# An attention and mixture-of-experts kernel: the exponential moves into the copy out of PSUM, and the list of steps is a new one

## The chip, the cores and the metric

The kernel runs on one core of a Trainium2 chip. The metric is the device time of one execution in microseconds (us). Engines are named as the profile names them: PE is TensorE's matmul side and PEld its weight loads, DVE is VectorE, ACT is ScalarE, POOL is GpSimd, SP is SyncE, which here only issues DMAs.

## The reference

```python
def _attn_ref(q, k, v):                       # q, k, v: 8 batches, 8 heads, 576 tokens, 64 wide, float32
    q_c = q.reshape(B, H, nc, chunk, D)       # nc = 9 chunks of 64 tokens; so are k_c, v_c
    scores = scale * np.matmul(q_c, k_c.transpose(0, 1, 2, 4, 3))      # scale = 1/8
    scores = scores - np.max(scores, axis=-1, keepdims=True)
    attn = np.exp(scores)
    attn = attn / (np.sum(attn, axis=-1, keepdims=True) + 1e-09)
    out = np.matmul(attn, v_c)
...
def _moe_ref(x, w_group, w_expert, w1, w2):   # x: 4608 tokens, 512 wide
    g_logits = x @ w_group                    # softmax over 4 groups, argmax: one group per token
    ...
        e_logits = xg @ w_expert[g]           # softmax over the group's 4 experts, argmax: one expert
        ...
            h = np.maximum(xg[mask_e] @ w1[g, e], 0.0)                 # 512 to 1024
            ye = h @ w2[g, e]                                          # 1024 to 512
            out[tok_idx] = (g_w[mask_g][mask_e] * e_w[mask_e])[:, None] * ye
```

## The kernel before, in words

The first part is attention with the routing of the tokens, the second runs the experts over the routed tokens. The second part ("units", one expert with up to 256 tokens each) is the same code before and after. The change lies in the first part.

Attention is cut into 36 tiles of 128 tokens: two chunks of 64 tokens, all eight heads. Each tile t goes through steps that have one letter each.

- **Q** loads the q and k of two tiles into a buffer `qk` (three buffers in turn); **V** loads the v of one tile with two or more copies into one of three blocks (`w1r`, `w2r`, `vg`; the first two hold weights later). Both go through SP's queue.
- **a** (`stage_a`, even numbers) turns q and k of a tile on PE, 16 transposes into a PSUM tile `tp`, of which there are two. ACT and DVE copy the halves to `qT` and `ktb` (line 419).
- **b** (`stage_b`) multiplies q with k into the PSUM tile `sc`, of which there is one. **s** (`stage_sub`) takes the row maxima on DVE (`m`) and writes the differences to `pr` in SBUF, which frees `sc`.
- **e** (`stage_exp`, line 452) takes the exponential of `pr` in place on ACT, with the scale of 1/8.
- **c** (`stage_ct`) turns `pr` on PE into a `tp`, often together with the output `x` of an earlier tile, and ACT copies it to `pT` (line 468).
- **p** (`stage_pv`) multiplies `pT` with v into the PSUM tile `o`; the v has a column of ones, so that a row of `o` also carries the row's sum. **n** (`stage_norm`) divides by it on DVE and writes `x`.
- **x** copies the turned `x` to `xT` on ACT (line 513). For every four tiles, steps written as digits and l, m and E follow: the router's logits, the choice of the expert, the rank of each token. **o** (on POOL) scatters the tokens to the experts' rows in HBM.
- **Z** fills spare rows in HBM from a tile of zeros, `pad` (five copies of 257 KB on SP's queue). P, j, J, X, U, L, H, D, W, w, y, F and R load and prepare the weights and run the first layer of the first expert.

No planner decides the order of these steps at run time or build time. `ORDER` is a string with all of them, and `run(ORDER)` records them one after the other; on each engine the instructions stand in this order, and wait for each other through semaphores. On SP's queue each copy besides waits until the copy eight before it has landed. An `a` with an odd number only forces a copy of the tile before it that is still owed; where nothing is owed it records nothing.

Of the kernel before, what the change touches and what calls it, by code (L numbers as in the profile page):

```python
# [13 lines left out]
AF = mybir.ActivationFunctionType  # L14
# [25 lines left out]
E1 = E + 1  # L40
NB0, NL0 = 2, 3
PB = (1, 3)
ORDER = ("a15 Q0 a19 a0 Q1 a6 a2 C0 G0 Q2 b0 a4 a11 a3 s0 a57 o0 a5 a13 b1 V0 e0 V2 a8 s1 c0 e1 b2 V1 a10 V3 p0 Q3 V7 G1"
# [17 lines left out]
FOUR = 16  # L61
VB = (0, 1, 0, 1, 0, 2, 1, 2, 2)
WHY = "the value comes from a table that the kernel builds within these bounds"
# [47 lines left out]
def moe_kernel(tc, q, k, v, w_group, w_expert, w1, w2, cst, out):  # L111
    nc = tc.nc
    w1 = w1.rearrange("g e d f -> (g e) d f")
    w2 = w2.rearrange("g e f d -> (g e) f d")
    with ExitStack() as ctx:
# [20 lines left out]
        x1 = xpool.tile([P, NG, XW], F32, name="x1", tag="x1")  # L136
# [7 lines left out]
        e0 = wpool.tile([1, 1], I32, name="e0")  # L144
# [88 lines left out]
        def prep_lo(i, eng=nc.gpsimd):  # L233
            h, l, r = prep_part(i, True)
            eng.tensor_sub(l, r, h.bitcast(F32))
# [5 lines left out]
        with ExitStack() as c1:  # L241
# [27 lines left out]
            st, TL = {}, NT - 1  # L269
# [81 lines left out]
            def flip(*parts):  # L351

                pt = banks().rearrange("p r (s c t) -> p r s c t", s=2, c=4)
                for i, f in enumerate(parts):
                    for c in range(4):
                        for r in range(2):
                            nc.tensor.transpose(pt[:, r, i, c], f(c)[HALF[r]], ident[HALF[r], HALF[r]])  # L357
                return [pt[:, :, i].rearrange("p r c t -> p c r t") for i in range(len(parts))]
# [88 lines left out]
                more(3)  # L447
                s["pr"] = pr

            def stage_exp(t):  # L450
                pr = st[t]["pr"]
                nc.scalar.activation(pr, pr, AF.Exp, scale=0.125)

            done = []

            def turned(t):
                o = st[t]["x"]
                return lambda c: o[:, c * P:(c + 1) * P]

            def stage_ct(t):  # L460
                pr = st[t]["pr"]
                parts = [lambda c: pr[:, c].rearrange("p x k -> p (x k)")]
                if done and done[0] <= t - 2:
                    o = done.pop(0)
                    parts.append(turned(o))
                pts = flip(*parts)
                pT = apool.tile([P, 4, P], F32, name="pT")
                nc.scalar.copy(pT.rearrange("p c (r t) -> p c r t", r=2), pts[0])
                st[t]["pT"] = pT
                if len(pts) > 1:  # L470
                    owed["x", o] = made[0], lambda: copy_x(o, pts[1])
# [37 lines left out]
            def copy_x(t, pt):  # L509
                g, i = divmod(t, NG)  # L510
                if i == 0:
                    st["xT", g] = xtpool.tile([P, 4, NG * P], F32, name="xT")
                nc.scalar.copy(st["xT", g][:, :, i * P:(i + 1) * P].rearrange("p c (r t) -> p c r t", r=2), pt)

            def stage_e1(g):
                xT = st["xT", g]
                lt = bank(g >= GL - 1)
                for c in range(4):
                    apart(mate[0], nc.tensor.matmul(lt[32 * c:32 * c + 32, :], lhsT=wg[:, c, :], rhs=xT[:, c, :], start=True, stop=True))
                st["lt", g] = lt, mate[0]  # L520

            def stage_lts(g):
                lts = xtpool.tile([P, 512], F32, name="lts")
                lt, h = st["lt", g]
                apart(h, nc.scalar.copy(lts, lt))
                st["lts", g] = lts

            def stage_e2(g):
                lts = st["lts", g]
                lg = lgk  # L530
                for i in range(NG):
                    nc.tensor.matmul(lg[:, i * 20:i * 20 + 20], lhsT=lts[:, i * P:(i + 1) * P],  # L532
                                     rhs=cs[:, C_SEL:C_SEL + 20], start=True, stop=True)
                st["lg", g] = lg
                routing.append(route(g))
# [249 lines left out]
            def prep2_lo(i, eng=nc.gpsimd):  # L785
                eng.tensor_sub(late2(4 + i // 2)[:, i % 2], w2r[i // K2][:, i % K2], hi2(0, i).bitcast(F32))
# [7 lines left out]
            def more(n=1):  # L794

                for _ in range(n):
                    while routing and next(routing[0], True):
                        routing.pop(0)
# [25 lines left out]
            def run(seq):  # L824
                g = dict(P=prep_hi, j=prep_lo, J=lambda i: prep_lo(i, nc.vector), X=first_x, U=first_xl, E=exponent, L=first_l1, H=first_hi, D=first_lo, W=prep2_hi, w=prep2_lo, y=lambda i: prep2_lo(i, nc.vector), F=first_loads, R=reload, V=load_v, C=load_cst,
                         Q=load_qk, G=load_wg, Z=prefill, a=stage_a)
                f = dict(o=stage_o, b=stage_b, s=stage_sub, c=stage_ct, e=stage_exp, p=stage_pv, n=stage_norm, x=stage_xt)
                for z in seq.split():
                    if z[0] == "m":
                        more(int(z[1:]))  # L830
                    elif z[0] in g:
                        g[z[0]](int(z[1:]))
                    elif z[0] == "1":
                        stage_e1(int(z[1:]))
                    elif z[0] == "l":
                        stage_lts(int(z[1:]))
                    elif z[0] == "2":
                        stage_e2(int(z[1:]))
                    elif z[0] == "3":
                        stage_e3(int(z[1:]))  # L840
                    elif 0 <= int(z[1:]) < NT:
                        f[z[0]](int(z[1:]))

            with tc.manual_schedule(engines={mybir.EngineType.PE, mybir.EngineType.DVE, mybir.EngineType.Activation, mybir.EngineType.SP, mybir.EngineType.Pool}):
                run(ORDER)
                while due:
# [22 lines left out]
        co, a, na, s4, thr, end = ft(2, "co"), ft(RPE, "a"), ft(2, "na"), ft(4, "s4"), ft(1, "thr"), ft(1, "end")  # L869
        ge, ff, ee = ft(U, "ge"), ft(U, "ff"), ft(E1, "ee")  # L870
        mk, rw = (ft(2 * U, n).rearrange("p (a u) -> p a u", a=2) for n in ("mk", "rw"))
        nd, thr2, bo, rv, rp, cd, pr = ft(1, "nd"), ft(1, "thr2"), ft(1, "bo"), ft(2, "rv"), ft(1, "rp"), ft(2, "cd"), ft(1, "prow")
        a64, nh, lf, th2 = ft(RPE, "a64"), ft(1, "nh"), ft(1, "lf"), ft(1, "th2")
# [814 lines left out]
```

## Time and profile before

| what | value |
|---|---|
| median of 3 runs (range) | 626.41 us (626.09 to 626.8) |
| profiled execution: time, and span of its instructions | 624.71 us, 623.1 us |
| mean granted clock of TensorE | 0.989 of full speed |
| ACT, busy time of the exponentials (line 452) | 22.4 us in 36 instructions |

The span runs from the first instruction to the last. The attention part fills about its first 183 us; from there the units run, with PE busy almost all of the time. An engine's busy time says little by itself; what counts is which wait ends last in a stretch.

### The profile page before, as it was taken

How to read it: one execution, taken by the hardware profiler on the slowest of the kernel's cores; microseconds unless marked ns; L12 is line 12 of the kernel's file. 1: busy time of each engine (PE TensorE's matmuls, PEld its weight loads, DVE VectorE, ACT ScalarE, POOL GpSimd, SP SyncE). 2: the span in 40 equal slices, each digit the busy share in tenths (PEclk: the TensorE clock that was granted, in tenths of full speed). 3: DMA queues.
4: the chain of work that ended last, by engine and by line, in shares of the span. 5: the costliest groups of instructions: out<-in, count | busy, mean ns of one | idle time of the engine just before them, and what ended most of it. 6: DMA issues, size and time to landing. Idle time of an engine off the chain costs nothing.

```text
span 623.1 us, 15370 instructions
## 1 busy us (share of the span) xinstructions
PE 593.3 (95%) x4882; PEld 502.0 (81%) x4883; DVE 428.8 (69%) x718; ACT 343.4 (55%) x521; POOL 220.6 (35%) x427
## 2 busy tenths in 40 slices
PE   3889999998999999999999999999999999999995
PEld 2777788777788888889888898888889888888884
DVE  4868889878868967427588876564844888966321
ACT  2878888888643835226375763534434575653311
POOL 9102555678861413113225232221311324323120
PEclk9889999999989999999999999999999999999998
DMA  9998999998548969213659667171721868741110
GB/s 224 239 280 227 285 284 277 273 259 250 180 181 262 395 206 351 85 51 95 243 229 343 241 243 266 62 291 43 272 99 38 304 241 277 288 166 67 34 37 31
DMA packets 104589, 128.00 MB, mean 205 GB/s; under 512 B 49438, under 2 KB 72222, under 8 KB 104544
## 3 DMA queue, kind: packets, MB, share of 16 engines
q1 hardware_dynamic: 93504, 92.71, 48.7%
q0 software_dynamic: 11040, 34.69, 15.6%
q8 instruction: 27, 0.44, 0.3%
q14 instruction: 18, 0.15, 0.1%
HBM read 106.23 MB, written 21.54 MB: 205 GB/s over the span
## 4 chain that ended last, share of the span: by engine, by line
PE 83%; DMA 6%; DVE 3%; ACT 3%; issue 3%; SPq 2%; DVEq 0%; POOL 0%; ACTq 0%; POOLq 0%
PE py L1047 29%; PE ph L1033 14%; PE ph L1015 7%; PE pxt L1033 6%; PE tp L357 5%; PE o L480 4%; PE sc L435 4%; DMA qk<-in_k_dram 3%; PE lgk L1033 3%; PE py L1064 2%; PE pxt L933 2%; DMA qk<-in_q_dram 2%; PE py L988 2%; PE lgk L532 1%; ACT qT L419 1%
## 5 line engine op out<-in xcount | busy, mean ns | idle before, releaser
L1589 POOL DMA_INDIRECT out_dram<-xl,io x37 | 41.6, 1125 | 155.4 <-DVE xl L1292 146.6
L1033 PE MATMUL ph<-xt,w1h 128*128 128x512 f32 (+1 forms) x280 | 73.2, 383 | 0.5 <-DVE htl L1345 0.5
L1223 ACT ACTIVATE hth<-ph 128x512 fp32r<-128x512 f32 (+1 forms) x28 | 16.1, 575 | 104.1 <-PE ph L1033 104.1
L1302 DVE TENSOR_TENSOR w1l<-w1r,w1h 128x2048 fp32r<-128x2048 f32 x28 | 64.0, 2291 | 8.5 <-ACT w1h L1199 7.5
L1047 PE MATMUL py<-w2h,hth 128*128 128x512 f32 x264 | 67.9, 399 | 0.0
L1047 PE MATMUL py<-w2h,htl 128*128 128x512 f32 x264 | 65.2, 389 | 0.0
L1306 DVE TENSOR_TENSOR w2l<-w2r,w2h 128x1024 fp32r<-128x1024 f32 x52 | 60.3, 1217 | 0.6 <-ACT w2h L1241 0.4
L1047 PEld LDWEIGHTS py<-w2h,htl 128*128 128x128 f32 x264 | 49.6, 188 | 10.3
L1047 PE MATMUL py<-w2l,hth 128*128 128x512 f32 x228 | 57.4, 390 | 0.0
L1047 PEld LDWEIGHTS py<-w2h,hth 128*128 128x128 f32 x264 | 47.3, 188 | 10.2 <-ACT hth L1277 1.2
L1199 ACT CAST w1h<-w1r 128x2048 fp32r<-128x2048 f32 x28 | 53.2, 1909 | 2.9 <-issue 1.5
L1033 PEld LDWEIGHTS ph<-xt,w1h 128*128 128x128 f32 x280 | 48.3, 189 | 6.7 <-DVE htl L1345 0.7
L1292 DVE TENSOR_SCALAR xl<-py,io 128x512 f32<-128x512 f32 x33 | 24.6, 748 | 42.0 <-PE py L1047 41.7
L1203 ACT CAST w2h<-w2r 128x2048 fp32r<-128x2048 f32 x28 | 52.3, 1929 | 0.0
L1047 PEld LDWEIGHTS py<-w2l,hth 128*128 128x128 f32 x228 | 42.8, 188 | 9.5
L1583 POOL COPY ion<-x1r 128x2 int32<-128x2 int32 x22 | 6.2, 281 | 119.0 <-PE pxt L933 119.0
L1274 ACT ACTIVATE xl<-ph 128x512 f32<-128x512 f32 x16 | 9.6, 599 | 69.3 <-PE ph L1015 69.3
L1033 PEld LDWEIGHTS ph<-xt,w1l 128*128 128x128 f32 x280 | 42.6, 189 | 4.9 <-DVE w1l L1302 0.3
L419 ACT COPY qT<-tp 64x512 f32<-64x512 f32 x56 | 36.7, 655 | 15.9 <-PE tp L357 14.6
L1033 PE MATMUL ph<-xt,w1l 128*128 128x256 f32 (+1 forms) x280 | 44.0, 278 | 0.1
L1333 DVE TENSOR_TENSOR xl<-ph,xl 128x512 f32<-128x512 f32 (+1 forms) x28 | 18.5, 661 | 35.2 <-ACT xl L1223 33.9
L357 PE MATMUL tp<-cs,qk 64*128 64x64 f32 x576 | 28.3, 242 | 13.6 <-DMA qk<-in_q_dram 8.6
(322 smaller groups left out, 1314.3 us busy)
## 6 DMA issues: line engine op xcount, KB each, us to landing
w2r<-in_moe_w_dram SPq DMA_DIRECT2D x30, 1024.0 KB, 7.5
w1r<-in_moe_w_dram SPq DMA_DIRECT2D x29, 1024.0 KB, 4.9
x1r<-xs POOLq DMA_DIRECT2D x38, 257.0 KB, 3.3
qk<-in_q_dram SPq DMA_DIRECT2D x15, 512.0 KB
qk<-in_k_dram SPq DMA_DIRECT2D x15, 512.0 KB
w1r<-in_v_dram SPq DMA_DIRECT2D x24, 128.0 KB
w2r<-in_v_dram SPq DMA_DIRECT2D x24, 128.0 KB
w1r<-in_moe_w_dram POOLq DMA_DIRECT2D x3, 1024.0 KB, 12.4
```

What stands on the lines that cost most here:

```text
L357: nc.tensor.transpose(pt[:, r, i, c], f(c)[HALF[r]], ident[HALF[r], HALF[r]])
L419: y.append((nc.vector.tensor_copy if not i and (z or a and FOUR <= n < 8 * B) else nc.scalar.copy)(to, at))
L435: nc.tensor.matmul(sc[HALF[c], hp], lhsT=st["T", u, 0][:, hp, c0 + j:c0 + j + CH], rhs=kt[:, hp, :, k0 + j:k0 + j + CH], start=True, stop= ...
L480: nc.tensor.matmul(o[HALF[c], hp // 2, hp % 2 * 2 * W:hp % 2 * 2 * W + 2 * W], lhsT=pT[:, hp, HALF[c]], rhs=s["va"][:, c, hp].rearrange("p ...
L1015: m = pe.matmul(ph[n], a_[:, c, 0:P], w_[:, c, n * 512:(n + 1) * 512], start=(i == 0), stop=(i == 11))
L1033: m = pe.matmul(o2 if i < 4 else o[:, 0:n], (w1l if i > 3 else w1h)[:, c, f * P:(f + 1) * P], both[:, c, :, 0:n] if i < 4 else xth()[:, c, ...
L1047: m = pe.matmul(py[j], a_[:, f, half[j]], w_(b, f), start=(i == 0), stop=(i == 23))
L1199: lambda b, s, j: ac.copy(wt[b][0][:, s], w1r[j]), K1, js)
L1203: lambda b, s, j: ac.copy(wt[b][2 + j], w2r[j]), K2)
L1302: lambda b, s, j: ve.tensor_sub(wt[b][1][:, s], w1r[j], wt[b][0][:, s].bitcast(F32)), K1, js)
L1306: m = ve.tensor_sub(wt[b][4 + 2 * j + i], w2r[j][:, 2 * i:2 * i + 2], wt[b][2 + j][:, 2 * i:2 * i + 2].bitcast(F32))
L1589: gp.indirect_dma_start(out, bass.IndirectOffsetOnAxis(ap=io[0:n, j, 0:1].bitcast(I32), axis=0), yb[0:n, j, :], None, bounds_check=N - 1, ...
```

## The change

`stage_exp` goes. `stage_ct` now turns the differences themselves, and the copy out of PSUM becomes an activation: ACT reads `tp`, applies the scale and the exponential, and writes `pT`. The letter e disappears from the list of steps, and the list is another one.

```diff
-ORDER = ("a15 Q0 a19 a0 Q1 a6 a2 C0 G0 Q2 b0 a4 a11 a3 s0 a57 o0 a5 a13 b1 V0 e0 V2 a8 s1 c0 e1 b2 V1 a10 V3 p0 Q3 V7 G1"
...
+ORDER = ("Q0 a5 a0 Q1 a6 a2 b0 C0 Q2 a19 V0 V2 V1 x2 a31 a61 V3 Q3 a4 G0 m1 x33 a8 V7 s0 V5 b1 c0 s1 b2 a10 s2 p0 Q4 a3 G1"
...
-            def stage_exp(t):
-                pr = st[t]["pr"]
-                nc.scalar.activation(pr, pr, AF.Exp, scale=0.125)
-
...
-                nc.scalar.copy(pT.rearrange("p c (r t) -> p c r t", r=2), pts[0])
+                nc.scalar.activation(pT.rearrange("p c (r t) -> p c r t", r=2), pts[0], AF.Exp, scale=0.125)
...
-                f = dict(o=stage_o, b=stage_b, s=stage_sub, c=stage_ct, e=stage_exp, p=stage_pv, n=stage_norm, x=stage_xt)
+                f = dict(o=stage_o, b=stage_b, s=stage_sub, c=stage_ct, p=stage_pv, n=stage_norm, x=stage_xt)
```

Line numbers after the change are five lower.

**ACT, the first tiles.** This is ACT's queue from the first copy into `ktb` to the second tile's `pT`, before:

```order
L419 COPY ktb_131<-tp 64x4x128
L419 COPY qT<-tp 64x4x128 x2
L419 COPY ktb_131<-tp 64x4x128
L452 ACTIVATE pr<-pr 128x512
L419 COPY qT<-tp 64x4x128 x2
L468 COPY pT<-tp 128x512
L452 ACTIVATE pr<-pr 128x512
L419 COPY ktb_132<-tp 64x4x128
L419 COPY qT<-tp 64x4x128 x2
L468 COPY pT<-tp 128x512
```

and after, from the same copy:

```order
L418 COPY ktb_131<-tp 64x4x128
L418 COPY qT<-tp 64x4x128 x2
L802 CAST tri<-cs 128x128
L803 CAST base<-cs 2x16
L418 COPY qT<-tp 64x4x128 x2
L418 COPY ktb_131<-tp 64x4x128
L463 ACTIVATE pT<-tp 128x512
L418 COPY ktb_132<-tp 64x4x128
L418 COPY qT<-tp 64x4x128 x2
L463 ACTIVATE pT<-tp 128x512
```

The activations of `pr` are gone, and each `pT` is written by an activation; two small casts stand later.

**SP, up to the sixth q and k.** The rows below end with the pair of q and k that is called Q5, for tiles 10 and 11; the pair further up is Q4. Before:

```order
L805 DMA wg<-in_moe_w_expert_dram 128x4x4 x2
L290 DMA qk<-in_q_dram 128x4x256
L290 DMA qk<-in_k_dram 128x4x256
L311 DMA w2r<-in_v_dram 64x8x64 x2
L819 DMA xs<-pad 128x514 x2
L311 DMA w2r<-in_v_dram 64x8x64 x2
L819 DMA xs<-pad 128x514
L311 DMA w2r<-in_v_dram 64x8x64 x2
L290 DMA qk<-in_q_dram 128x4x256
L290 DMA qk<-in_k_dram 128x4x256
```

and after:

```order
L310 DMA w2r<-in_v_dram 64x8x64 x4
L289 DMA qk<-in_q_dram 128x4x256
L289 DMA qk<-in_k_dram 128x4x256
L800 DMA wg<-in_moe_w_expert_dram 128x4x4
L310 DMA w2r<-in_v_dram 64x8x64 x2
L800 DMA wg<-in_moe_w_expert_dram 128x4x4
L310 DMA w2r<-in_v_dram 64x8x64 x2
L814 DMA xs<-pad 128x514
L289 DMA qk<-in_q_dram 128x4x256
L289 DMA qk<-in_k_dram 128x4x256
```

The same 16 copies of v stand ahead of Q5 (eight of them for `w1r`, further up in both), but one copy of `pad` in place of three; the other two follow Q5.

**SP, tiles 12 to 23.** The rows go from v for `w2r` past the pairs Q10 (the first q and k) and Q11 to Q13 (the last). Before:

```order
L311 DMA w2r<-in_v_dram 64x8x64 x6
L290 DMA qk<-in_q_dram 128x4x256
L290 DMA qk<-in_k_dram 128x4x256
L311 DMA w1r<-in_v_dram 64x8x64 x2
L290 DMA qk<-in_q_dram 128x4x256
L290 DMA qk<-in_k_dram 128x4x256
L311 DMA w1r<-in_v_dram 64x8x64 x6
L290 DMA qk<-in_q_dram 128x4x256
L290 DMA qk<-in_k_dram 128x4x256
L311 DMA vg<-in_v_dram 64x8x64 x8
```

and after:

```order
L310 DMA w2r<-in_v_dram 64x8x64 x2
L289 DMA qk<-in_q_dram 128x4x256
L289 DMA qk<-in_k_dram 128x4x256
L310 DMA w2r<-in_v_dram 64x8x64 x4
L310 DMA w1r<-in_v_dram 64x8x64 x2
L289 DMA qk<-in_q_dram 128x4x256
L289 DMA qk<-in_k_dram 128x4x256
L310 DMA w1r<-in_v_dram 64x8x64 x6
L310 DMA vg<-in_v_dram 64x8x64 x6
L289 DMA qk<-in_q_dram 128x4x256
L289 DMA qk<-in_k_dram 128x4x256
```

Q10 has passed four copies of v for `w2r`, and Q13 stands behind six copies of v for `vg` that followed it before.

## Rows read from the trace of the kernel before

**Rows 1.** Stretches: start:end, length, busy us (instructions) by engine; clock, DMA share, GB/s.
```profile
25.00:50.00 25.00, 21.27 (x372) 17.71 (x370) 18.70 (x38) 20.07 (x35) 0.00 (x0) 0.93 1.06 269
50.00:150.00 100.00, 96.47 (x1689) 79.03 (x1685) 86.94 (x209) 85.80 (x153) 59.77 (x168) 1.00 0.99 266
183.00:623.00 440.00, 432.75 (x2299) 369.52 (x2299) 284.34 (x376) 207.39 (x278) 119.20 (x189) 1.00 0.53 187
```

**Rows 2.** The chain that ended last: start, length, what.
```profile
34.37 8.11 DMA qk<-in_k_dram
...
71.93 5.64 DMA qk<-in_k_dram
...
121.51 11.18 DMA qk<-in_q_dram
```

**Rows 3.** Waits of PEld, 43 to 165 us: for whom, us in total, times, longest.
```profile
PEld tp L357 <- ACT ktb L419: 2.1, 4, 0.8
PEld tp L357 <- ACT xT L513: 1.8, 7, 0.4
PEld tp L357 <- ACT w2h L783: 1.7, 2, 0.9
PEld o L480 <- ACT pT L468: 1.6, 3, 0.8
PEld tp L357 <- ACT qT L419: 1.0, 2, 0.8
PEld sc L435 <- ACT pr L452: 0.8, 1, 0.8
```

**Rows 4.** Waits of PE, 43 to 183 us.
```profile
PE tp L357 <- ACT xT L513: 0.5, 2, 0.3
PE o L480 <- ACT pT L468: 0.5, 2, 0.3
PE tp L357 <- DMA qk<-in_k_dram: 0.4, 1, 0.4
```

**Rows 5.** ACT's groups: busy us, mean ns of one, idle before them.
```profile
L452 ACT ACTIVATE pr<-pr 128x512 f32<-128x512 f32 x36 | 22.4, 631 | 1.4 <-DVE pr L446 1.3
L468 ACT COPY pT<-tp 128x512 f32<-128x512 f32 x36 | 20.9, 586 | 10.2 <-PE tp L357 8.7 <-PE o L480 0.7 <-ACT lts L525 0.2
L1274 ACT ACTIVATE xl<-ph 128x512 f32<-128x512 f32 x16 | 9.6, 599 | 69.3 <-PE ph L1015 69.3
```

**Rows 6.** Timeline of the first 43 us: start, length, instructions, idle before and its end.
```profile
18.05 1.45 PE L435 MATMUL sc<-ktb,qT 128*64 128x128 f32 x16 [1.55 <-DVE pr L446]
...
40.14 0.46 PE L357 MATMUL tp<-cs,qk 64*128 64x64 f32 x8 [0.17 <-ACT xT L513]
...
42.53 1.55 PE L357 MATMUL tp<-cs,qk 64*128 64x64 f32 x24 [1.93 <-DMA qk<-in_k_dram]
```

**Rows 7.** SP's issues to DMA queues: start, length, copies.
```profile
27.50 1.09 SPq L819 DMA_DIRECT2D xs<-pad  x2
...
30.72 1.38 SPq L819 DMA_DIRECT2D xs<-pad  x1
...
34.37 0.51 SPq L290 DMA_DIRECT2D qk<-in_k_dram  x1
...
62.37 8.85 SPq L311 DMA_DIRECT2D w2r<-in_v_dram  x6
...
85.96 0.51 SPq L290 DMA_DIRECT2D qk<-in_k_dram  x1
86.56 9.75 SPq L311 DMA_DIRECT2D vg<-in_v_dram  x8
```

**Rows 8.** DMA issues: copies of the spare rows, KB each.
```profile
xs<-pad SPq DMA_DIRECT2D x5, 257.0 KB
```

**Rows 9.** PE's timeline where it first needs Q13 (the row of qk).
```profile
101.28 1.11 PE L480 MATMUL o<-w1r,pT 128*64 128x130 f32 x16
102.33 0.71 PE L357 MATMUL tp<-cs,qk 64*128 64x64 f32 x16
```

33 rows, old and new, of the table ORDER are left out of this document.

## The prediction

> **What bounds the kernel now.** I began with busy times by stretch [rows 1]. From 183 us on the code is the same in both kernels, and PE is busy for 432.75 of 440 us: that part keeps its length and only starts sooner or later. So the question is when the first 183 us end. Between 50 and 150 us the reader is to see four things almost full at once: PE 96.47 of 100, DVE 86.94, ACT 85.80, and the DMA engines at a share of 0.99 with 266 GB/s. No single one bounds; each waits for another now and then.
>
> Next I read the chain that ended last [rows 2]. Most of it is PE, but three long pieces are loads of q or k: one of 8.11 us that ends at 42.48, one of 5.64 us, one of 11.18 us. So the front of the kernel is set by what SP's queue brings, and the middle partly.
>
> Then I asked for whom PE waits. PE's own rows from 43 to 183 us put only 1.0 us on ACT's copies [rows 4]. Its weight loads, from 43 to 165 us, wait 9.0 us for ACT in the six groups shown, and 1.4 us in six smaller ones (`pT` 0.4, and five of 0.2), 10.4 us together [rows 3]. The two differ by ten, and the price of the whole change hangs on which is taken. Each small matmul here has its own weight load and cannot start without it, and ends of matmuls are modelled, so that an idle PE of some 0.2 us is covered in its rows. Between 50 and 150 us the weight loads are busy 79.03 us where PE shows 96.47 [rows 1]: there is more room than PE's rows say. I take 10.4 us as the most that ACT can give back there, and 1.0 us as the figure by PE's rows.
>
> The Trainium skill ("Trainium Kernel Development and Optimization", Performance Expectations) says the same of traces in general: matmul busy time is a bad measure because matmuls are pipelined, and the busy share of the weight loads a good one. By the matmul rows the term for ACT below would be at most 1.0 us; by the weight loads' rows it is up to 10.4. This trace's gap between 96.47 and 79.03 agrees with the page.
>
> **The change, step by step.**
>
> *The exponentials go.* 36 instructions of 631 ns, 22.4 us of ACT [rows 5]. From 50 to 150 us one is taken from ACT for each tile, some 24 tiles, so 24 x 0.63 = 15.1 us: ACT's 85.80 fall to 70.7, and its idle time doubles from 14.2 to 29.3. With twice the gaps in its queue I would expect about half of PE's waits for ACT to go, 5.2 us. But DVE, at 86.94, keeps all its work and is then the fuller of the two that empty PSUM; tiles that come faster meet it more often. I take 3.0 us, which is a choice; the bounds are 0 and 10.4.
>
> *The copy becomes an activation.* 36 copies of 586 ns [rows 5]. The trace has no exponential out of PSUM of this size. Bounds: 586 (as the copy), and 631, the exponential from SBUF. The nearest row is the Relu of line 1274, same size and out of PSUM, 599 ns. I take that: 13 ns x 36 = 0.5 us on ACT, at most 45 x 36 = 1.6. Only part of ACT's time reaches PE, 10.4 us of waits in 122 us; I put 0.1 us on the path (0 to 0.5).
>
> *The first tiles.* Without the exponential a tile's scores reach its `pT` some 0.6 us sooner, and in the new list PE turns the q and k of a further tile ahead of the second tile's scores, where it idled 1.55 us for DVE [rows 6]. I cost both at nothing, because what hides them is a load: PE is ready for Q5 at 40.14 and stands until 42.53 for its k [rows 6]. Whatever is won before waits there. If the load were not late, they would be worth up to about 2 us.
>
> *Q5 comes sooner.* SP's queue issues without a break up to Q5's k at 34.37 [rows 7], and the copies are the brake: a DMA share of 1.06 at 269 GB/s from 25 to 50 us [rows 1]. In the new list two of the three copies of `pad` stand behind Q5, and the 16 copies of v ahead of it are the same. That is 2 x 257 KB [rows 8] = 0.53 MB, at 269 GB/s 2.0 us. The issue times give nearly the same: two of three copies in 1.09 + 1.38 us [rows 7] are 1.6. I take 2.0 us. Bounds: 0, if Q4, which now stands behind two more copies of v, makes PE late instead; 3.7, if the granted clock, 0.93 in that stretch [rows 1], gives back its 7% of 25 us as well. I don't count on the clock, since PE still arrives before Q5 does. The two copies behind Q5 now stand ahead of Q6, but after 43 us PE's only wait for a k is one of 0.4 us [rows 4].
>
> *Q10 passes four copies of v.* Six copies take 8.85 us to issue [rows 7], so four are 5.9 us; the 0.4 us that PE waits for a k after 43 us [rows 4], at the end of the 5.64 us piece [rows 2], goes. Bounds 0 and 0.4.
>
> *Q13 falls behind six copies of v.* 9.75 us for eight [rows 7], so 7.3 us. Its k was issued at 85.96 [rows 7] and PE first needs it at 102.33 [rows 9]; the new issue is at about 93.3. PE will be there 2.0 + 0.4 and some 1.3 of the 3.0 us sooner, at 98.6. With 5.64 us from issue to landing [rows 2] it is there at 98.9, 0.3 us late. I count 0, and price the worse case below.
>
> *The end of the part.* Routing, first layer of the first expert and hand-over are the same instructions in nearly the same order; I count 0, with 1 us either way.
>
> **Sum.** -3.0 + 0.1 - 2.0 - 0.4 = -5.3 us. The profiled execution took 624.71 us, so 619.4. Its time lies 1.70 under the median of the runs, 626.41; so the runs should show 626.41 - 5.3 = **621.1 us**.
>
> **Rivals.**
>
> *The waits change their owner.* ACT's waits go, and PE waits for DVE, or for DMA, instead. For it: DVE is as full as ACT was, and the DMA share is 0.99 [rows 1]; then the 2.0 us of Q5 are also handed back at the next load. Against it: Q5's delay is a delay of copies that nothing needed early. Between nothing and the 0.4 of Q10 plus half of the 2.0 would be left, 0 to 1.4 us: about 625.7, no change that can be measured.
>
> *Q13 comes too late (slower).* If Q13's k takes the 11.18 us of the chain's third load [rows 2] and not 5.64, it lands at 93.3 + 11.2 = 104.5, 5.9 us after PE wants it. That eats the 5.3 us and 0.6 more; and after so long a stall the clock would fall as in the stretch of the earlier one, 0.93 for 25 us, another 1.75 [rows 1]. 626.41 + 2.3 = 628.7. It decides from a landing of some 11 us on. For it: the queue has eight copies under way, and six of them are now copies of v just issued. Against it: the chain's other two loads took 5.64 and 8.11 us; with 8.11 PE would wait 2.8 us, and the kernel would still be faster.
>
> *All of it.* Both doubts resolve well: PE's whole 10.4 us go and the clock's 1.75 are given back. -5.3 - 7.4 - 1.75 = -14.4, 612. Against it: PE is at 96.47 of 100 even so, and v and k must come at a rate that is already 266 GB/s. Half of the extra, some 616.5, is as far as I go.
>
> That the change does not do what it says can be left out: the activations of `pr` are gone from ACT's queue.
>
> **How the numbers follow.** A measurement of this kernel tells about 0.2% from no change, 1.25 us. Forecast, between 1.25 and 9 us gained: 0.67. All of it: 0.04. Waits that change their owner: 0.17. Q13 late: 0.12. So faster 0.71, same 0.17, slower 0.12. The range: below, 616.5 keeps half of the extra gain; above, 626.7 takes in the second case whole and cuts the third. The forecast's own range is 617.4 to 625.
>
> **What would show it.** ACT's groups: line 463 with 36 instructions at about 600 ns, no exponential of 128x512 besides; ACT's busy time some 22 us less. The wait for a k near 42.5 us ends near 40.5. The weight loads' waits for ACT's `ktb`, `pT` and `xT` are together a third less. The wait for Q10's k is gone, and one for a k near 98 us is below 1 us. From the start of the units to the end, 440 us as before. It would be wrong if PE's waits for DVE grow by what those for ACT lose, or if SP's queue shows a long wait for a buffer in front of a pair of q and k.

## The result, and the profile after

The changed kernel takes 628.76 us (median of 14 runs; the kernel before, run beside it, 624.1): a ratio of **1.0076 [1.0049, 1.0103]**. It is slower, where 621.1 us and faster was forecast (0.992 of the 626.41 us that were known then). In two later groups of runs the same kernel gave 1.0052 [1.0021, 1.0084] and 1.0067 [1.0039, 1.0095]. The profiled execution took 628.77 us, with a span of 627.1 us.

First the busy times by stretch, as in [rows 1] (stretch and its length; PE, PEld, DVE, ACT, POOL; granted clock, DMA share, GB/s):

```profile
25.00:50.00 25.00, 19.21 (x330) 15.74 (x332) 16.90 (x33) 14.96 (x25) 0.00 (x0) 0.93 0.95 248
50.00:150.00 100.00, 93.55 (x1645) 77.63 (x1643) 84.69 (x202) 72.76 (x125) 57.66 (x165) 0.99 1.03 265
183.00:623.00 440.00, 435.80 (x2328) 372.38 (x2323) 286.68 (x384) 207.91 (x280) 120.00 (x192) 1.00 0.54 188
```

Between 50 and 150 us ACT fell from 85.80 to 72.76 us, as meant. But PE fell too, from 96.47 to 93.55: it is idle 3 us more there, with ACT idle for 27 of 100 us. The DMA engines are as full as before.

The moved exponential has the size that was expected of it, 598 ns (the groups of ACT, as [rows 5]):

```profile
L463 ACT ACTIVATE pT<-tp 128x512 f32<-128x512 f32 x36 | 21.4, 598 | 19.6 <-PE tp L356 18.2 <-PE o L475 1.0
```

PE's weight loads wait less for ACT, too (43 to 165 us, as [rows 3]; smaller groups left out):

```profile
PEld tp L356 <- ACT xT L508: 3.2, 8, 0.8
PEld tp L356 <- ACT qT L418: 1.6, 2, 0.8
PEld tp L356 <- ACT ktb L418: 1.2, 4, 0.4
PEld tp L356 <- ACT pT L463: 1.1, 2, 0.8
```

With all groups of `xT`, `qT`, `ktb` and `pT` taken together that is 7.5 us where the kernel before had 7.3; what is gone is the exponential's share and nearly all of the weights' (`w2h`). The waits for ACT are about 8 us in all against 10.4.

Where the loss lies is told by one row of PE's timeline, the first matmul of the units. It stands in the kernel before at

```profile
199.42 1.12 PE L1033 MATMUL ph<-xt,w1h 128*128 128x512 f32 x4
```

and in the changed kernel at

```profile
203.42 1.12 PE L1028 MATMUL ph<-xt,w1h 128*128 128x512 f32 x4
```

4.0 us later, which is the whole difference of the spans (627.1 - 623.1): the units themselves are as long as before, and everything was lost in the attention part. This start of the units is used below as the yardstick for a trace. It holds for one execution only: three traces of the changed kernel lie 2.2 us apart (203.42, and 205.01 and 202.85 further below).

PE's timeline shows four places where it now stands. In each row the bracket is the idle time ahead and what ended it.

```profile
42.52 0.97 PE L356 MATMUL tp<-cs,qk 64*128 64x64 f32 x24 [0.96 <-DMA qk<-in_k_dram]
45.27 1.39 PE L514 MATMUL lgk<-xT,wg 128*32 128x512 f32 x8 [1.77 <-DMA wg<-in_moe_w_expert_dram]
...
112.72 0.40 PE L356 MATMUL tp<-cs,pr 64*128 64x64 f32 x6 [1.46 <-issue]
...
146.19 0.25 PE L356 MATMUL tp<-cs,qk 64*128 64x64 f32 x1 [0.83 <-DMA qk<-in_k_dram]
147.14 0.43 PE L356 MATMUL tp<-cs,qk 64*128 64x64 f32 x7 [0.71 <-DMA qk<-in_k_dram]
```

At 42.5 us it waits for Q5 as before. At 45.3 it waits for the last two copies of the router's weights. At 111.3 it stops in the middle of a group of eight transposes, for nothing that the profile names. At 146 to 147 it waits for Q17, the last q and k. None of the last three was in the prediction. The other two traces of this kernel show the same stop, but not the same waits after 43 us: after_again waits 1.1 us for the router's weights and not for Q17, after_third 2.5 and 1.9 us. SP's issues show why the two waits came:

```profile
19.32 3.06 SPq L807 DMA_DIRECT2D wg<-in_moe_w_group_dram  x1
...
34.24 0.60 SPq L289 DMA_DIRECT2D qk<-in_k_dram  x1
34.89 1.49 SPq L814 DMA_DIRECT2D xs<-pad  x2
36.42 3.31 SPq L800 DMA_DIRECT2D wg<-in_moe_w_expert_dram  x2
...
123.39 13.63 SPq L310 DMA_DIRECT2D vg<-in_v_dram  x8
137.11 2.21 SPq L299 DMA_DIRECT2D qk<-in_q_dram  x4
```

Q5's k is issued at 34.24 us, against 34.37 in [rows 7]: not 2 us sooner, though two pads moved behind it. The queue stood 3.06 us at a tiny copy of weights (G0), which the new list puts there. That is a part of it at most, for in the trace of after_third the stand is shorter and Q5's k still comes only 0.5 us sooner:

```profile
19.46 1.34 SPq L807 DMA_DIRECT2D wg<-in_moe_w_group_dram  x1
...
33.86 0.61 SPq L289 DMA_DIRECT2D qk<-in_k_dram  x1
```

Fewer bytes did not take less time. These are the stretches from 20 to 34.3 us, before and after (as [rows 1]):

```profile
20.00:34.30 14.30, 13.55 (x244) 11.73 (x240) 12.16 (x23) 13.34 (x22) 0.00 (x0) 0.93 1.05 259
20.00:34.30 14.30, 12.47 (x234) 10.82 (x236) 11.73 (x23) 10.46 (x17) 0.00 (x0) 1.00 0.90 215
```

At 215 instead of 259 GB/s some 0.63 MB less moved in the same time, about the two pads (0.53 MB) that were taken out.

The router's weights (G3, G4) now stand behind Q5 and two pads and are issued at 36.42, not 34.92. The new list also asks for them sooner: PE is ready for the first logits at 43.50 (45.27 - 1.77), where the kernel before starts them, without a wait, at

```profile
46.85 1.07 PE L519 MATMUL lgk<-xT,wg 128*32 128x512 f32 x8
```

Q17 stands behind eight copies of v that take 13.63 us to issue.

### The profile page after: what moved, and what is told of

Same layout as the page of the kernel before. It is cut to its first block, busy times and chain, and to the rows that moved or that the text cites. A ratio compares the mean times of both kernels' runs of the same rounds, so it can differ in the third digit from the quotient of the medians.

```text
span 627.1 us, 15330 instructions
## 1 busy us (share of the span) xinstructions
PE 592.1 (94%) x4882; PEld 500.3 (80%) x4883; DVE 431.0 (69%) x718; ACT 326.1 (52%) x485; POOL 221.1 (35%) x427
## 4 chain that ended last, share of the span: by engine, by line
PE 80%; DMA 5%; DVE 5%; issue 3%; SPq 3%; ACT 2%; POOL 1%; DVEq 0%; ACTq 0%; POOLq 0%
PE py L1042 29%; PE ph L1028 14%; PE ph L1010 7%; PE pxt L1028 6%; PE tp L356 4%; PE o L475 3%; DMA qk<-in_k_dram 3%; PE sc L434 3%; PE lgk L1028 3%; PE py L1059 2%; PE pxt L928 2%; PE py L983 2%; PE lgk L514 1%; SPq L299 1%; DMA wg<-in_moe_w_expert_dram 1%
## 5 line engine op out<-in xcount | busy, mean ns | idle before, releaser
L1584 POOL DMA_INDIRECT out_dram<-xl,io x37 | 39.7, 1072 | 157.0 <-DVE xl L1287 147.1
L1042 PEld LDWEIGHTS py<-w2h,htl 128*128 128x128 f32 x264 | 49.6, 188 | 10.3
L1042 PEld LDWEIGHTS py<-w2h,hth 128*128 128x128 f32 x264 | 47.3, 188 | 10.3 <-ACT hth L1272 1.2
L1028 PEld LDWEIGHTS ph<-xt,w1l 128*128 128x128 f32 x280 | 42.5, 189 | 4.9 <-DVE w1l L1297 0.3
```

What stands on the lines that cost most here:

```text
L1028: m = pe.matmul(o2 if i < 4 else o[:, 0:n], (w1l if i > 3 else w1h)[:, c, f * P:(f + 1) * P], both[:, c, :, 0:n] if i < 4 else xth()[:, c, ...
L1042: m = pe.matmul(py[j], a_[:, f, half[j]], w_(b, f), start=(i == 0), stop=(i == 23))
L1584: gp.indirect_dma_start(out, bass.IndirectOffsetOnAxis(ap=io[0:n, j, 0:1].bitcast(I32), axis=0), yb[0:n, j, :], None, bounds_check=N - 1, ...
```

## The experiments

Runs were made in five groups; the kernel before had medians of 635.0, 625.3, 625.9, 624.9 and 635.2 us in them, so ratios are compared within a group, and traces, where nothing else is said, from the groups near 625. What makes the other two groups slower was not tried; it lies in the attention part, for in the trace of fuse_old (group 1) the units start at 211.53 us and are as long as before. After each kernel stands its group.

### What the fusion is worth in the old list (groups 1 and 2)

**fuse_old**: the exponential moved, the old list without its letters e.

```diff
-ORDER = (new list)
+ORDER = (list of before, every e left out)
```

Expected: 

> The exponential moves into the copy out of PSUM, but the list of steps is that of before with the letter e struck out. Theory (the step itself helps, the new list loses): ACT loses 22 us, a third of PE's waits for it goes, Q17 stands ahead of v as before: 2 to 3 us faster than before, ratio 0.995 to 0.997. Rival (the step itself costs, since the exponential now lies between the turning and the product): not faster than before, ratio 1.000 to 1.005.

Measured: 1.0009 [0.9983, 1.0035]. The fusion by itself gains nothing that can be told, at most 1.1 us.

**sep_new**: the other half, the changed list with the old separate exponential.

Expected: 

> The new list, but with the exponential taken by itself as before (each e stands half way between its s and its c). Theory: the losses of the list stay and ACT is as full as before: 2 to 3 us slower than the changed kernel, ratio to before 1.010 to 1.013. Rival (the step itself costs): it comes back to before, ratio 0.998 to 1.002.

Measured: 1.0131 [1.0099, 1.0164]. That is 1.1% above new_q17 of the same group (1.0017, see below), the same list but for one load and with the exponential in the copy. PE's weight loads wait for ACT (43 to 165 us):

```profile
PEld tp L357 <- ACT xT L513: 6.4, 9, 1.3
PEld tp L357 <- ACT ktb L419: 5.9, 7, 1.5
...
PEld tp L357 <- ACT pr L452: 3.3, 4, 1.1
```

That is 15.6 us in three groups; `xT` and `ktb` have 6.4 of it in new_q17, `pr` none. The exponentials that cost nothing in the old list cost about 7 us in this one. Whether ACT's time is dear there or only the places, half way between s and c, were bad ones was not tried.

**fuse_act2**: ACT's time given back, without anything that waits for it.

```diff
+            def stage_exp(t):
+                nc.scalar.activation(idle[1], idle[0], AF.Exp, scale=0.125)
```

Expected: 

> The exponential on the way out of PSUM, in the old list of steps, and beside it the 36 old exponentials again, each on two scratch buffers that nothing else reads or writes: ACT has its 22 us back, but nothing waits for them. Theory 'ACT has slack in the attention part, what the kernel runs at there is set by PE and the loads': the ratio to the kernel before stays at the fusion's own 1.001, between 0.998 and 1.004. Theory 'ACT's time is worth something there, as the prediction had it (3.0 us, bounds 0 to 10.4)': 1.005 to 1.017.

Measured: 0.9982 [0.9957, 1.0006]. ACT's groups and the busy times from 50 to 150 us in its trace:

```profile
L453 ACT ACTIVATE idle<-idle 128x512 f32<-128x512 f32 x36 | 22.7, 632 | 0.2
```
```profile
50.00:150.00 100.00, 96.79 (x1695) 79.45 (x1695) 87.31 (x208) 85.85 (x153) 59.59 (x168) 1.00 1.00 267
```

ACT is as full as before the change (85.85), and the kernel is no slower than the one before; fuse_q5 below, with ACT unburdened, has the same 0.9982 in its group. In the old list ACT's exponentials lie beside other work, as far as a quarter of a percent can tell.

**fuse_pe2** and **fuse_pad2**: the same probe on PE and on SP's queue.

```diff
+                        for _ in range(2 if hp < 2 else 1):
                             nc.tensor.matmul(sc[HALF[c], hp], ...
```
```diff
+                for _ in range(2):
                     nc.sync.dma_start(xs[i * P:(i + 1) * P, :], pad)
```

Expected: 

> As the fusion in the old list, with half of the scores' matmuls made twice (the second writes the same numbers over the first): PE gets 576 records of 290 ns and less more, some 20.9 us with their weight loads' share, by the score rows of the kernel before between 50 and 150 us (26.21 us for 384 of 290 rows by half). Theory 'PE sets the pace of the attention part': 12 to 21 us more, 1.020 to 1.034. Theory 'the loads set it, PE only waits less': under 6 us more, 1.000 to 1.010.

Measured: 1.0164 [1.013, 1.0198], 10.3 us on 625.27 (the medians, 633.59 and 625.27, lie 8.3 us apart). In the trace the two groups of PE's score matmuls grew by 288 matmuls (not 576, as the expectation has it) and 16.0 us:

```profile
L435 PE MATMUL sc<-ktb,qT 128*64 128x128 f32 x768 | 51.4, 282 | 2.4 <-DVE pr L446 2.4
L435 PE MATMUL sc<-kT,qT 128*64 128x128 f32 x96 | 6.3, 279 | 0.0
```

against 37.3 and 4.4 us in the kernel before:

```profile
L435 PE MATMUL sc<-ktb,qT 128*64 128x128 f32 x512 | 37.3, 290 | 2.7 <-DVE pr L446 2.5
L435 PE MATMUL sc<-kT,qT 128*64 128x128 f32 x64 | 4.4, 279 | 0.0
```

So half to two thirds of what PE gets comes out at the end. Neither expectation had it: PE sets much of the pace, not all.

Expected: 

> As the fusion in the old list, with each of the five copies of the pad made twice: 1.3 MB more in SP's queue before tile 11, 4.8 us at 266 GB/s. Theory 'the loads set the pace of the first half': 3 to 5 us more, 1.005 to 1.009. Theory 'PE does, and the loads only now and then': under 1.5 us, 1.000 to 1.003.

Measured: 1.0329 [1.0283, 1.0376], 20.6 us (17.8 by the medians), about four times the 4.8 us that was expected of the bytes. The second copy to the same rows waits for the first, and the queue stands with it (waits of SP):

```profile
SPq L815 <- DMA xs<-pad: 20.2, 5, 5.4
```

So this run says nothing of bytes, but much of the queue. The five waits, 20.2 us, lie between 28 and 70 us; three of the five pads stand ahead of Q5 and its tiles 10 and 11, not all five as the expectation has it. The profiled execution took 641.49 us, 16.2 above the median of the kernel before. PE shows it most in one wait for v:

```profile
PE o L475 <- DMA w2r<-in_v_dram: 11.9, 1, 11.9
```

The granted clock is lower as well, 0.82, 0.84 and 0.86 in the three stretches of 25 us from 25 to 100 us, against 0.93, 1.00 and 1.00 before, so that a part of the loss may be the clock's.

**fuse_q5** (group 3): the prediction's step on Q5 by itself.

```diff
-... b4 a14 Z4 n1 m1 c3 s4 Z1 ... V6 Z0 s5 V4 ... n3 Q5 c5
+... b4 a14 Q5 Z4 n1 m1 c3 s4 Z1 ... V6 Z0 s5 V4 ... n3 c5
```

Expected: 

> The fusion in the old list (1.0009 by itself), with Q5 moved ahead of three copies of the pad and of V6 and V4, some 5 us of SP's queue: the prediction's step 'Q5 comes sooner' by itself and larger. By the prediction PE's stand for Q5's k near 42.5 us goes and 2 us are won: 0.995 to 0.998. Theory 'the queue as a whole sets the pace, so that the wait only passes to the next load or to a copy of v': 0.999 to 1.003.

Measured: 0.9982 [0.9946, 1.0017], no gain that can be told. The interval would also hold a gain of 2 us; the trace speaks against one. SP issues Q5's k at 28.11 us, 6 us sooner, and PE's stand for it is gone; but the v that was passed is late instead (PE's timeline):

```profile
41.20 1.45 PE L475 MATMUL o<-w2r,pT 128*64 128x130 f32 x16 [2.49 <-DMA w2r<-in_v_dram]
```

PE starts the first logits at 46.75 us, where the kernel before does at 46.85: nothing was won up to there.

### Which part of the new list loses (groups 1 to 4)

**new_q17** and **new_both** (group 1), and again in group 4: the changed kernel with Q17 ahead of V28, alone and with G3 and G4 ahead of Q5; **new_wg**: G3 and G4 alone. **q17_late** (group 2): the kernel before, with Q17 behind V31.

```diff
-... Q16 V28 ... V31 ... E0 x26 a66 Q17 P6
+... Q16 Q17 V28 ... V31 ... E0 x26 a66 P6
```
```diff
-... Q5 Z1 b5 x12 a35 Z0 G3 a16 n2 s5 G4
+... G3 G4 Q5 Z1 b5 x12 a35 Z0 a16 n2 s5
```

Expected (new_q17): 

> The changed kernel with Q17 ahead of the eight copies of v for tiles 28 to 31 on SP's queue, as in the list of before. Theory: PE's wait for Q17 near 145 us goes, and with it the slow clock behind it: 3 to 5 us faster than the changed kernel, ratio to before 1.000 to 1.003. Rival (a wait for v of tile 28 takes its place, or the end of the part waits for something else): as the changed kernel, ratio 1.006 to 1.009.

Expected (new_both): 

> As new_q17, and the four experts' router weights (two copies, G3 and G4) ahead of Q5 on SP's queue. Theory: the first logits no longer wait for them near 44 us: 1 to 2 us faster than new_q17, ratio to before 0.997 to 1.001. Rival (Q5 then comes as much later): as new_q17.

Measured in group 1: 1.0017 [0.9995, 1.004] and 1.0008 [0.9982, 1.0035]. I took this for proof that Q17 is most of the loss, although the changed kernel itself was not in that group.

Expected (q17_late): 

> The kernel before with one step of its list moved: Q17, the last loads of q and k, behind the eight copies of v of V28 to V31 instead of ahead of them, as the changed list has it. Theory 'Q17's place is most of the loss': 1.004 to 1.007. Theory 'Q17 is late only together with the fusion or the rest of the new list': 0.998 to 1.002.

Measured: 0.9979 [0.9957, 1.0001]. The old list does not mind a late Q17. Its queue gets there sooner, by SP's issues:

```profile
119.44 11.30 SPq L311 DMA_DIRECT2D vg<-in_v_dram  x8
130.84 2.74 SPq L300 DMA_DIRECT2D qk<-in_q_dram  x4
133.63 3.22 SPq L300 DMA_DIRECT2D qk<-in_k_dram  x4
```

The same eight copies of v begin 4 us sooner than in the changed kernel, and Q17's q is issued at 130.84, not 137.11. So Q17's place alone is not the cause. To settle it the changed kernel was run beside the repairs on one chip:

Expected (after_third): 

> The changed kernel unaltered, as the measure of the three run with it on the same chip: 1.004 to 1.009, from its two earlier ratios 1.0076 and 1.0052.

Expected (new_q17_again): 

> The changed kernel with Q17 ahead of the eight copies of v of V28 to V31, as once before on another chip (1.0017). Theory 'Q17 is most of the loss': 1.000 to 1.003. Theory 'the loss is spread over the places where the loads come late (router weights near 45 us, PE's pause near 112 us, Q17), and each by itself is worth a third': 1.003 to 1.006.

Expected (new_wg): 

> The changed kernel with the last two copies of the router weights, G3 and G4, ahead of Q5, and Q17 as the changed list has it. Theory 'Q17 is most of the loss': 1.004 to 1.009, as the changed kernel. Theory 'the loss is spread': 1.003 to 1.006.

Expected (new_both_again): 

> Both moves together, as once before on another chip (1.0008): 0.999 to 1.003 by either theory; by 'spread' about 0.002 under Q17 alone, by 'Q17' level with it.

Measured: 1.0067 [1.0039, 1.0095] for the changed kernel, then 1.0058 [1.0021, 1.0095], 1.007 [1.0039, 1.0101] and 1.0056 [1.002, 1.0091]. No repair recovers what can be told. The theory "Q17 is most of the loss" falls; its support had come from a group without the changed kernel in it. The same two kernels have 1.0017 and 1.0008 in group 1 and 1.0058 and 1.0056 in group 4, so that what a list costs depends on the group. What happens instead is to be seen in new_both_again, where the router's weights are in time and a later pair of q and k (Q8) is late, behind eight copies of v and two pads (PE's timeline):

```profile
60.59 0.46 PE L356 MATMUL tp<-cs,qk 64*128 64x64 f32 x8 [0.80 <-DMA qk<-in_q_dram]
61.93 0.69 PE L356 MATMUL tp<-cs,qk 64*128 64x64 f32 x8 [0.88 <-DMA qk<-in_k_dram]
```

### The queue's order against the engines' order (groups 3 and 5)

The two orders were crossed. **new_oldloads**: the changed list, but the first place that loads anything loads what the old list loads first, and so on. **old_newloads**: the reverse.

```diff
-Q0 a5 a0 Q1 a6 a2 b0 C0 Q2 a19 V0 V2 ...
+Q0 a5 a0 Q1 a6 a2 b0 C0 G0 a19 Q2 V0 ...
```

Expected (after_again): 

> The changed kernel once more, unaltered, so that its own ratio stands beside the three kernels run with it on the same chip: 1.005 to 1.010 by every theory.

Expected (new_oldloads): 

> The changed kernel with its list of steps for the engines, but with SP's queue in the old order: the first place in the list that loads anything loads what the old list loads first, and so on, so that SP's queue is that of the old list row for row. Theory 'the order of the loads is the loss': 0.997 to 1.002. Theory 'the new order of the engines' own steps is the loss': 1.005 to 1.010.

Expected (old_newloads): 

> The other way round: the fusion with the old list for the engines' steps, and SP's queue in the order of the changed list (V20 alone stands one load sooner, because its product comes sooner). Theory 'the order of the loads is the loss': 1.004 to 1.009. Theory 'the new order of the engines' own steps is the loss': 0.998 to 1.003.

Measured: 1.0052 [1.0021, 1.0084] for the changed kernel, 0.9997 [0.996, 1.0034] with the old queue, and 0.9966 [0.9938, 0.9994] for the reverse, in which G0, which also writes the columns of ones beside v, came behind tile 0's product, so that tile 0 is divided by the wrong sums. G0 also carries small copies on ACT and POOL, which moved with it. The runs of group 3 put against each other (ratio of the mean times, runs drawn anew for the interval) give 1.0044 [1.0021, 1.0071] for the changed kernel over new_oldloads, and 1.0069 [1.0046, 1.0092] over old_newloads. Both were run once more, the reverse with G0 in time:

Expected (new_oldloads_again): 

> The changed list for the engines with SP's queue in the old order, once more (0.9997 [0.996, 1.0034] before). Theory 'SP's order as a whole is the loss, though none of its moves by itself is': 0.997 to 1.002 again, clear of the changed kernel's 1.0039 to 1.0095 on the third chip. Theory 'the engines' own order is part of it': 1.002 to 1.006.

Expected (old_newloads2): 

> The old list for the engines with SP's queue in the changed order, V20 and G0 one load sooner. In the run of old_newloads G0, which also writes the columns of ones beside v, stood behind tile 0's product, so that tile 0 was divided by the wrong sums there; here it stands ahead of it. Theory 'the changed queue costs only together with the changed order of the engines': 0.996 to 1.002 as before (0.9966). Theory 'the changed queue costs by itself': 1.003 to 1.007.

Measured: 0.9986 [0.9958, 1.0015] and 1.0002 [0.997, 1.0035]; the changed kernel itself was not in this group, one of the two slower ones, and in the other, group 1, its repairs lost next to nothing too. So neither order was seen to lose by itself, and of group 3 alone it can be said that the two together lose; there the reverse had its wrong sums. The units start, by PE's timeline of the run after_again, at

```profile
205.01 1.13 PE L1028 MATMUL ph<-xt,w1h 128*128 128x512 f32 x4
```

by that of after_third at

```profile
202.85 1.13 PE L1028 MATMUL ph<-xt,w1h 128*128 128x512 f32 x4
```

and by that of new_oldloads, with the old queue, at

```profile
199.37 1.13 PE L1028 MATMUL ph<-xt,w1h 128*128 128x512 f32 x4
```

The last is the kernel before to 0.05 us (199.42); that it is so close is chance, as single traces scatter by more. Same engines' order, same fusion, old queue: the loss is gone, in this trace as in the ratios. The repaired kernels start at 203.30 (new_q17_again), 201.96 (new_wg) and 202.15 (new_both_again), which shows no repair: new_wg's profiled execution, 627.45 us, lies 2.9 below its own median. The trace of old_newloads errs the other way (627.05 us, median 624.66). Its units start at

```profile
201.44 1.12 PE L1028 MATMUL ph<-xt,w1h 128*128 128x512 f32 x4
```

and PE waits 8.8 us for q and k in it, 2.7 of them for Q17. What it does not wait for are the router's weights. They are issued no sooner than in the changed kernel (37.50 us), but the old list asks for them later (PE's timeline):

```profile
47.21 1.06 PE L514 MATMUL lgk<-xT,wg 128*32 128x512 f32 x8
```

At this place the loss needs both orders: a load that comes later and a step that comes sooner.

PE's stop at 111 us belongs to this as well. It comes in all three traces of the changed kernel (1.46, 2.12, 1.74 us) and in new_wg (1.74), always after the second of the same eight transposes. In new_oldloads PE has the same instructions and goes through (its timeline):

```profile
108.55 0.41 PE L356 MATMUL tp<-cs,pr 64*128 64x64 f32 x8
108.89 1.07 PE L514 MATMUL lgk<-xT,wg 128*32 128x512 f32 x8
```

The transfers of the DMA engines hold a queue of the kind "instruction" (packets, MB, share). In the changed kernel one block of it moves between 110 and 112 us, as PE stops at 111.26:

```profile
q8 instruction: 1, 0.02, 3.5%
```

and in new_oldloads between 104 and 106 us, some 3 us before PE is at that place:

```profile
q8 instruction: 1, 0.02, 3.0%
```

In the four traces that stop, the block has moved by 111.4, 114.0, 111.2 and 109.7 us, and PE goes on 1.4 to 1.5 us later each time. It looks as if PE ran out of instructions because their block was late among the loads. That is argued from the times, not shown by a run.

## Why the prediction was wrong, step by step

**The exponentials go, -3.0 us: wrong, it is 0 as far as can be told.** fuse_old, fuse_act2 and the two runs with the old queue all have ratios within 0.2% of the kernel before. The step that failed is the choice of the weight loads' rows (10.4 us of waits for ACT) over PE's own (1.0 us, [rows 3, 4]). The page of the Trainium skill that I cited for that choice ("Trainium Kernel Development and Optimization", Performance Expectations) calls matmul busy time a bad measure, and the weight loads' busy share a good one, of how close a kernel is to roofline. It does not speak of waits; I stretched it to them. Here PE's own rows were nearer to the truth, for 16.0 us of additional matmul time made the kernel 8 to 10 us longer, and 22.7 us of additional ACT time made it no longer. The lower bound of that term, 0, was in the sum's bounds, and I had the reason for it in front of me: PE at 96.47 of 100.

**The activation in place of the copy, +0.1:** its length is right, 598 ns where 599 was estimated; 0.1 us on the path is less than a run can tell.

**The first tiles, 0:** right. Their first `pT` is begun 1.9 us sooner (19.95 against 21.87 us), the next ones 1.6 and 0.4, and PE then waits for Q5 and the router's weights.

**Q5 comes sooner, -2.0 us: wrong, it is 0, for two reasons.** I priced the pads' bytes that left the queue ahead of Q5 at a fixed 269 GB/s, and the queue did not keep its rate: 215 GB/s from 20 to 34.3 us where it had 259. G0, in front of which the queue stood 3.06 us in one trace and 1.34 in another, came in besides. And the gain would not have lasted. fuse_q5 has Q5 6 us sooner and wins nothing that can be told, since a v is late instead. The sum treated "PE waits for Q5" as one load's lateness, where the queue as a whole was late.

**Q10, -0.4, and Q13, 0:** Q13 came in time as forecast, and the slower rival that was built on it did not happen. The 0.4 us for Q10 are gone, but PE's waits for k did not shrink: 5.1, 2.6 and 3.9 us in the three traces of the changed kernel from 12 to 190 us, against 3.4 before.

**What the sum left out** is the sign. I costed three moves in SP's queue and put the others at nothing without a reason: G0, the router's weights, Q17. The last two are late by one to 2.5 us in a trace, and where one was put right another load was late (fuse_q5, new_both_again). All together make 0.5 to 0.8%: in group 3 that vanishes when the queue alone is put back.

**The rivals.** "The waits change their owner" had the right mechanism and the wrong size: the waits went from ACT to the loads, but there was no gain for them to cancel, and they became more. Its 0.17 and the slower case's 0.12 were too little for a change that reorders a queue whose copies are the brake.

**The end of the part, 440 us as before:** right.

What stays open: why the changed queue costs nothing that can be told under the old engines' order (old_newloads, old_newloads2). That the two orders depend on each other is shown at one place, the router's weights; which other instruction needs which load sooner was not traced out one by one. That the changed list has less slack for ACT is a guess from sep_new. And the stop of PE at 111 us was not tried by itself.

## What to carry to other kernels

Before pricing an engine's lighter load, ask what the engine that sets the pace would do with the time: a probe that gives the lightened engine its old work back, with nothing waiting for it, tells it in one run. Where one queue issues all loads, price its whole order against when each load is needed, and not a single move in it; here a load that was made earlier made another late. And a repair is only compared with the broken kernel in the same group of runs.

## What was not expected of the hardware

20.2 us in which one queue waited for its own earlier copies to the same rows came out as 16 to 21 us at the end of the kernel, more than 550 us later; a lower granted clock, 0.82 to 0.86 from 25 to 100 us, may have a part in it. And PE stopped for 1.5 to 2.1 us in the middle of a group of transposes with nothing to wait for, in every trace of one kernel, and went through the same instructions in another that differs in SP's queue alone but for G0's small copies.
